# Five matmuls instead of six in units 2 and 14 of seven batches of a Fourier-mixing and maxout kernel

## The chip, the cores and the metric

The kernel runs on one core of one Trainium2 chip. The metric is the time of one execution on the device, in microseconds; runs of the kernel before took 401.41, 401.44 and 402.31 us, median 401.44. A core has a matrix engine (TensorE, PE in the profile, with its weight loads as PEld), a vector engine (VectorE, DVE), a scalar engine (ScalarE, ACT), GpSimd (POOL) and a queue engine for transfers (SyncE, SP). Each runs its own instructions in order, and they wait for one another by semaphores. Matmul results lie in PSUM, eight banks of 512 float32 columns by 128 partitions; all else lies in SBUF.

## What is computed

Eight batches of 3072 tokens with 256 features go through a two-dimensional Fourier transform, of which the real part is kept, and then through a layer that takes the largest of three products and a second matrix:

```python
batch, seq, dim = (8, 3072, 256)            # x; d_ff = 768
X = np.fft.fft(x, axis=1)
X = np.fft.fft(X, axis=2)
x = X.real.astype(np.float32).reshape(B * S, D)
h = np.maximum(np.maximum(x @ w1, x @ w2), x @ w3)
return h @ w_out
```

## The kernel before, in words

**Algebra.** The transform along the features is folded into the weights. For each batch the kernel makes two tables, tE and tO, of 128 rows by 1536 token columns (half the sequence; the other half are the mirrored tokens, which have the same even part and an odd part of the other sign). The weights w2 - w1 and w3 - w1 are kept transformed as gE and gO, so that pse = gE x tE + gO x tO is the first layer's difference for a token, and gD, which is gO times -2 with one row left out by the factor dif, turns it into the value for the mirrored token by one more product, pse + gD x tO. The hidden value is max(pse2, pse3, 0), and w1's part comes in later, as a linear term through gw.

**Units.** A batch has three blocks of 512 token columns and six groups (jc) of 128 hidden rows, so 18 units; the loop at the end runs over all 144 with one number g. A unit gives hp (tokens) and hm (mirrored tokens), 128 x 512 each in bf16. There are two kinds:
- Six matmuls: begin calls unit_plus (two products into pse2, two into pse3; L436, L437) and unit_out (ScalarE's Relu of pse2 into stmp, L450; VectorE's maximum with pse3 into hp, L451). finish calls unit_minus (one product with gD into each bank, L444) and unit_out again, into hm.
- Five matmuls ("split": odd g from 7 on). third, two units ahead, makes e3 = gE[1] x tE (L758) and d3 = gD[1] x tO (L760). ScalarE writes odd3 = -0.5 x d3 (L762), VectorE writes even3 = vb x wcol + e3 (L763; vb is row 0 of tO on all partitions), and POOL makes plus3 = even3 + odd3 and minus3 = even3 - odd3 in bf16 (L767). begin then makes pse2 alone (L774, L775), and VectorE takes max(pse2, 0, plus3) into hp (L776); finish adds gD[0] x tO (L444) and takes max(pse2, 0, minus3) into hm (L788).

**Order.** The order on every engine is the order of the program, written out by hand. In iteration g: if the unit before is split, its finish; then begin(g); then the finish of the unit before if it wasn't split; then third(g + 2) if g + 2 is split; scatter (POOL's indirect stores); ten steps of the second layer (l2_some: the products po and pl, L483 and L475, and hp and hm by w_out, L460, into po; then VectorE's ot = po + even, L488, and the stores); then what plan has for this unit of the next batch: the first transform (s, L369, evicted by ScalarE, L372) in units 1 and 2, the tables (k, L411, evicted by ScalarE, L413) in units 12 to 15, mirrored copies by ScalarE (L129), loads by POOL.

**Buffers.** PSUM is dealt out as: ps_f, a ring of three banks, which e3, d3, pl, the products of s and k, and a few others share; ps_l1, two banks for pse2; ps_w3, one bank for pse3 of even units; ps_o, two banks for po and for pse3 of odd units of six matmuls. s_pool holds three each of even3, odd3, plus3 and minus3; hp and hm have two sets, ot six.

Of the kernel before, what the change touches and what calls it, by code (L numbers as in the profile page):

```python
# [9 lines left out]
FP32 = mybir.dt.float32  # L10
BF16 = mybir.dt.bfloat16
INT32 = mybir.dt.int32
AX = mybir.ActivationFunctionType
ALU = mybir.AluOpType
# [36 lines left out]
def kernel(  # L51
# [9 lines left out]
    nc = tc.nc  # L61

    B, S, D = x.shape
# [3 lines left out]
    TOKB = 512  # L67
    NHALF = 1536
    UNITS = 3 * NJC
# [104 lines left out]
    for r in (0, 6, 11):  # L174
        n = {0: 6, 6: 5, 11: 4}[r]
# [25 lines left out]
    def scal(out, in0, s1, op0, s2=None, op1=None, eng=None):  # L201
# [8 lines left out]
                                   op0=ALU.mult, op1=ALU.add)  # L210
# [3 lines left out]
                                   op0=ALU.mult, op1=ALU.add)  # L214
# [5 lines left out]
                                   op0=ALU.mult, op1=ALU.add)  # L220
# [7 lines left out]
    half = gen.tile([128, 256], FP32, tag="half")  # L228
# [7 lines left out]
    for fc in range(2):  # L236
        scal(pf[:, fc:fc + 1], pidx, float(128 * fc), ALU.add)
        nc.vector.scalar_tensor_tensor(
            out=vm[:, fc * 256:(fc + 1) * 256].rearrange("p (k c) -> p k c", c=128),
            in0=dvec.unsqueeze(1).to_broadcast([128, 2, 128]), scalar=pf[:, fc:fc + 1],  # L240
            in1=half.rearrange("p (k c) -> p k c", c=128), op0=ALU.mult, op1=ALU.add)
# [12 lines left out]
                          in_=par.unsqueeze(1).to_broadcast([128, 2, 2]))  # L254
# [365 lines left out]
    for (s0, s1) in HALVES:  # L620
        for h in range(2):
            load_x(1, s0, s1, h)
        if s0 == 0:
            nc.gpsimd.dma_start(out=wout_bf.rearrange("p (jc c) -> p jc c", jc=NJC),
                                in_=moe_w_out.rearrange("(jc p) c -> p jc c", jc=NJC))
# [18 lines left out]
    for u in range(3):  # L644
# [7 lines left out]
                       in1=adj.unsqueeze(1).to_broadcast([128, B, 12]), op=ALU.add)  # L652
# [8 lines left out]
    s_pool = ctx.enter_context(tc.tile_pool(name="sums", bufs=3))  # L661
# [79 lines left out]

    sums = {}

    def is_split(g):
        return g % 2 == 1 and 7 <= g < B * UNITS

    def operands(g):
        b, u = divmod(g, UNITS)
        blk, jc = divmod(u, NJC)
        mm = mixes[b]  # L750
        ts = slice(blk * TOKB, (blk + 1) * TOKB)
        return slice(jc * 128, (jc + 1) * 128), mm.tE[:, ts], mm.tO[:, ts], mm.vb[:, ts], jc

    def third(g):

        js, te, to, vb, jc = operands(g)
        e3 = ps_f.tile([128, TOKB], FP32, name="e3", tag="ps")
        nc.tensor.matmul(e3, gE[1][:, js], te, start=True, stop=True)  # L758
        d3 = ps_f.tile([128, TOKB], FP32, name="d3", tag="ps")
        nc.tensor.matmul(d3, gD[1][:, js], to, start=True, stop=True)  # L760
        even3, odd3 = (s_pool.tile([128, TOKB], FP32, name=n, tag=n) for n in ("even3", "odd3"))
        nc.scalar.activation(out=odd3, in_=d3, func=AX.Copy, scale=-0.5)  # L762
        nc.vector.scalar_tensor_tensor(out=even3, in0=vb, scalar=wcol[:, jc:jc + 1], in1=e3,  # L763
                                       op0=ALU.mult, op1=ALU.add)
        sums[g] = [s_pool.tile([128, TOKB], BF16, name=n, tag=n) for n in ("plus3", "minus3")]
        for dst, op in zip(sums[g], (ALU.add, ALU.subtract)):
            nc.gpsimd.tensor_tensor(out=dst, in0=even3, in1=odd3, op=op)  # L767

    def begin(g, dst):

        js, te, to, _, jc = operands(g)
        if is_split(g):
            pse2 = ps_l1.tile([128, TOKB], FP32, name="pse2", tag="pse2")
            nc.tensor.matmul(pse2, gE[0][:, js], te, start=True, stop=False)  # L774
            nc.tensor.matmul(pse2, gO[0][:, js], to, start=False, stop=True)  # L775
            nc.vector.scalar_tensor_tensor(out=dst, in0=pse2, scalar=0.0, in1=sums[g][0],  # L776
                                           op0=ALU.max, op1=ALU.max)
            return (pse2,)
        pses = unit_plus(te, to, jc, TOKB, *((ps_o, "po") if g % 2 else (ps_w3, "pse3")))
        unit_out(pses, dst, TOKB)  # L780
        return pses

    def finish(g, pses, dst):

        js, te, to, _, jc = operands(g)
        unit_minus(pses, to, jc)
        if is_split(g):
            nc.vector.scalar_tensor_tensor(out=dst, in0=pses[0], scalar=0.0, in1=sums.pop(g)[1],  # L788
                                           op0=ALU.max, op1=ALU.max)
        else:  # L790
            unit_out(pses, dst, TOKB)

    prev = None
    for g in range(B * UNITS):
# [13 lines left out]
        if prev is not None and is_split(prev[0]):  # L808
            finish(*prev)
            prev = None  # L810
# [4 lines left out]
        for lead in (1, 2):  # L815
            if is_split(g + lead) and (lead == 1) == (g + lead == 7):
                third(g + lead)
# [46 lines left out]
```

## Time and profile before

| | us |
|---|---|
| median of three runs | 401.44 |
| the profiled execution | 403.04 |
| its span, first to last instruction | 400.8 |
| PE busy | 381.5 |
| DVE busy | 319.2 |
| POOL busy | 324.6 |
| ACT busy | 260.2 |

A row of the profile names the line of the kernel, the engine, the operation, the tile written and those read, their shapes, the count, then busy time and the mean of one. The main groups that the change touches, with the idle time just before them and what ended most of it:

```profile
L450 ACT ACTIVATE stmp<-pse 128x512 bf16<-128x512 f32 x150 | 89.8, 600 | 66.3 <-PE pse L444 46.3
L767 POOL TENSOR_TENSOR plus<-even,odd 128x512 bf16<-128x512 f32 x69 | 87.9, 1274 | 34.6 <-DVE even L763 28.4
L444 PE MATMUL pse<-tO,gD 128*128 128x512 bf16 x219 | 70.9, 379 | 0.6
L763 DVE SCALAR_TENSOR_TENSOR even<-vb,wcol,e 128x512 f32<-128x512 bf16 x69 | 51.0, 739 | 0.0
L762 ACT ACTIVATE odd<-d 128x512 f32<-128x512 f32 x69 | 41.3, 598 | 6.4 <-PE pl L475 0.4
```

A matmul's row is longer (379 ns) than the distance to the next one's start, because matmuls overlap in the array. Lines of the order of time give the start in us, the length in us, the engine, line, operation, tiles, and in brackets the engine's idle time before it with its releaser.

### The profile page before, as it was taken

The page shows a single profiled execution, that of the slowest core. Times are in us where ns is not written, and L with a number is a line of the kernel's source. Part 1 is how long each engine was busy: PE and PEld are TensorE (multiplying, and loading weights), DVE is VectorE, ACT ScalarE, POOL GpSimd, SP SyncE. Part 2 cuts the span into 40 slices and gives each one's busy share as a digit, 9 for nine tenths or more (in the row PEclk, how much of TensorE's full clock was granted, in tenths as well). Part 3 has the DMA queues.
Part 4 walks back from the last instruction along what each step waited for, and adds up shares of the span by engine and source line. Part 5 has one row for each costly group of instructions (what it writes and reads, how often), then busy time and mean ns, then how long its engine had stood idle before and what let it go on. Part 6 is the DMA issues. An engine that isn't in the chain of part 4 may idle for free.

```text
span 400.8 us, 8295 instructions
## 1 busy us (share of the span) xinstructions
PE 381.5 (95%) x2691; PEld 236.9 (59%) x2739; DVE 319.2 (80%) x542; ACT 260.2 (65%) x466; POOL 324.6 (81%) x408
## 2 busy tenths in 40 slices
PE   6679899999999999999999999999999999999994
PEld 2245456656665666656665666656665666666673
DVE  5978877877887887877887887877887887887982
ACT  1576779768865778568865778568775546544420
POOL 6465479788998899898988899898978798778993
PEclk9799999999999999999999999999999999999999
DMA  7989978395765958395875958394432653322234
GB/s 116 190 160 190 176 196 168 110 156 151 187 146 112 197 146 161 111 188 129 178 152 106 194 150 172 109 180 124 151 105 78 140 150 108 93 74 52 88 87 137
DMA packets 69532, 56.30 MB, mean 140 GB/s; under 512 B 35040, under 2 KB 64992, under 8 KB 68292
## 3 DMA queue, kind: packets, MB, share of 16 engines
q0 software_dynamic: 23552, 26.53, 35.4%
q1 hardware_dynamic: 44898, 28.70, 27.3%
q10 hardware_dynamic: 1040, 0.56, 0.5%
q8 instruction: 21, 0.34, 0.3%
q14 instruction: 21, 0.17, 0.2%
HBM read 38.15 MB, written 31.71 MB: 174 GB/s over the span
## 4 chain that ended last, share of the span: by engine, by line
PE 81%; DMA 8%; DVE 4%; ACT 3%; issue 2%; SPq 1%; POOL 0%; DVEq 0%; POOLq 0%; ACTq 0%
PE po L460 29%; PE pse L444 11%; PE pse L436 8%; PE pse L437 6%; PE po L483 4%; PE pse L774 4%; PE d L760 3%; PE e L758 3%; PE pse L775 3%; DMA yb<-db 3%; PE ps L369 3%; PE ps L411 2%; PE pl L475 2%; DMA xt<-in_x_dram 2%; ACT tb L372 2%
## 5 line engine op out<-in xcount | busy, mean ns | idle before, releaser
L450 ACT ACTIVATE stmp<-pse 128x512 bf16<-128x512 f32 x150 | 89.8, 600 | 66.3 <-PE pse L444 46.3
L570 POOL DMA_INDIRECT out_dram<-ot,rows_m x92 | 102.3, 1112 | 17.9 <-issue 7.8
L767 POOL TENSOR_TENSOR plus<-even,odd 128x512 bf16<-128x512 f32 x69 | 87.9, 1274 | 34.6 <-DVE even L763 28.4
L767 POOL TENSOR_TENSOR minus<-even,odd 128x512 bf16<-128x512 f32 x69 | 87.6, 1270 | 0.0
L460 PE MATMUL po<-wout_bf,hp 128*128 128x256 bf16 x576 | 86.1, 273 | 0.4
L776 DVE SCALAR_TENSOR_TENSOR hp<-pse,plus 128x512 bf16<-128x512 f32 x69 | 47.7, 691 | 46.1 <-PE pse L775 19.0
L460 PE MATMUL po<-wout_bf,hm 128*128 128x256 bf16 x576 | 78.6, 273 | 0.1
L460 PEld LDWEIGHTS <-hp 128*128 128x128 bf16 x576 | 56.4, 98 | 26.1
L444 PE MATMUL pse<-tO,gD 128*128 128x512 bf16 x219 | 70.9, 379 | 0.6
L460 PEld LDWEIGHTS <-hm 128*128 128x128 bf16 x576 | 56.4, 98 | 16.3
L488 DVE TENSOR_TENSOR ot<-po,even 128x512 f32<-128x512 f32 x92 | 63.0, 684 | 0.0
L451 DVE TENSOR_TENSOR hp<-pse,stmp 128x512 bf16<-128x512 f32 x75 | 51.6, 688 | 9.6 <-ACT stmp L450 7.8
L436 PE MATMUL pse<-tE,gE 128*128 128x512 bf16 x148 | 56.0, 378 | 2.0 <-DVE tE L413 0.5
L451 DVE TENSOR_TENSOR hm<-pse,stmp 128x512 bf16<-128x512 f32 x75 | 51.7, 689 | 7.2 <-ACT stmp L450 3.9
L763 DVE SCALAR_TENSOR_TENSOR even<-vb,wcol,e 128x512 f32<-128x512 bf16 x69 | 51.0, 739 | 0.0
L437 PE MATMUL pse<-tO,gO 128*128 128x512 bf16 x128 | 48.5, 379 | 0.2 <-issue 0.2
L788 DVE SCALAR_TENSOR_TENSOR hm<-pse,minus 128x512 bf16<-128x512 f32 x69 | 47.3, 685 | 1.2 <-PE pse L444 0.4
L762 ACT ACTIVATE odd<-d 128x512 f32<-128x512 f32 x69 | 41.3, 598 | 6.4 <-PE pl L475 0.4
L129 ACT COPY xt<-xt 64x762 bf16<-64x762 bf16 (+1 forms) x48 | 40.2, 838 | 1.1
L372 ACT CAST tb<-ps 128x512 bf16<-128x512 f32 x46 | 24.8, 589 | 22.9 <-PE ps L369 22.9
L444 PEld LDWEIGHTS <-gD 128*128 128x128 bf16 x219 | 21.4, 98 | 23.1 <-issue 5.0
L483 PE MATMUL po<-gw,tO 128*128 128x512 bf16 x86 | 32.7, 380 | 0.0
(156 smaller groups left out, 463.8 us busy)
## 6 DMA issues: line engine op xcount, KB each, us to landing
yb<-db SPq DMA_DIRECT2D x7, 833.0 KB
xt<-in_x_dram POOLq DMA_DIRECT2D x14, 384.0 KB, 8.6
out_dram<-ot SPq DMA_DIRECT2D x55, 96.0 KB
out_dram<-ot SPq DMA_DIRECT2D x64, 64.0 KB
db<-tb SPq DMA_DIRECT2D x21, 192.0 KB
vb<-vd SPq DMA_DIRECT2D x23, 128.0 KB
xt<-in_x_dram POOLq DMA_DIRECT2D x7, 400.0 KB, 8.6
xt<-in_x_dram POOLq DMA_DIRECT2D x7, 368.0 KB, 8.8
```

The source lines that it names most:

```text
L436: nc.tensor.matmul(pse[:, 0:n], gE[i][:, js], te, start=True, stop=False)
L437: nc.tensor.matmul(pse[:, 0:n], gO[i][:, js], to, start=False, stop=True)
L444: nc.tensor.matmul(pse, gD[i][:, js], to, start=False, stop=True, skip_group_check=True)
L450: nc.scalar.activation(out=stmp[:, 0:n], in_=pses[0][:, 0:n], func=AX.Relu)
L451: nc.vector.tensor_tensor(out=dst, in0=src3, in1=stmp[:, 0:n], op=ALU.max)
L460: nc.tensor.matmul(po, hcols(jc), wout_bf[:, jc * 256:(jc + 1) * 256], start=False, stop=(jc == NJC - 1), skip_group_check=True)
L483: nc.tensor.matmul(po, to[:, cp], gw[:, 256:768], start=True, stop=True)
L488: nc.vector.tensor_tensor(out=ot.rearrange("p (h c) -> p h c", h=2), in0=po.rearrange("p (h c) -> p h c", h=2), in1=lin.unsqueeze(1).to_br ...
L570: stored(nc.gpsimd.indirect_dma_start(out, bass.IndirectOffsetOnAxis(ap=rows_m[0:128 - lo, at_row: at_row + 1], axis=0), ot[lo:128, 256:51 ...
L763: nc.vector.scalar_tensor_tensor(out=even3, in0=vb, scalar=wcol[:, jc:jc + 1], in1=e3, op0=ALU.mult, op1=ALU.add)
L767: nc.gpsimd.tensor_tensor(out=dst, in0=even3, in1=odd3, op=op)
L776: nc.vector.scalar_tensor_tensor(out=dst, in0=pse2, scalar=0.0, in1=sums[g][0], op0=ALU.max, op1=ALU.max)
```

## The change

Units 2 and 14 of batches 1 to 7, 14 units in all, become units of five matmuls. They are even, so third runs for them in units 0 and 12, and from unit 1 to 3 and 13 to 15 three such units follow one another. For these units alone the sums are made otherwise: ScalarE's odd3 and POOL's two operations are left out, and VectorE makes plus3 = -0.5 x d3 + even3 and minus3 = 0.5 x d3 + even3 itself, reading d3 from its bank. Since is_split holds for them, their finish comes before the begin of the next unit, and they use no pse3 and no stmp.

```diff
+    def on_dve(g):
+        return g >= UNITS and g % UNITS in (2, 14) and g < B * UNITS
+
     def is_split(g):
-        return g % 2 == 1 and 7 <= g < B * UNITS
+        return (g % 2 == 1 and 7 <= g < B * UNITS) or on_dve(g)
...
-        even3, odd3 = (s_pool.tile([128, TOKB], FP32, name=n, tag=n) for n in ("even3", "odd3"))
-        nc.scalar.activation(out=odd3, in_=d3, func=AX.Copy, scale=-0.5)
+        even3 = s_pool.tile([128, TOKB], FP32, name="even3", tag="even3")
+        if not on_dve(g):
+            odd3 = s_pool.tile([128, TOKB], FP32, name="odd3", tag="odd3")
+            nc.scalar.activation(out=odd3, in_=d3, func=AX.Copy, scale=-0.5)
         nc.vector.scalar_tensor_tensor(out=even3, in0=vb, scalar=wcol[:, jc:jc + 1], in1=e3,
                                        op0=ALU.mult, op1=ALU.add)
         sums[g] = [s_pool.tile([128, TOKB], BF16, name=n, tag=n) for n in ("plus3", "minus3")]
+        if on_dve(g):
+            for dst, half in zip(sums[g], (-0.5, 0.5)):
+                nc.vector.scalar_tensor_tensor(out=dst, in0=d3, scalar=half, in1=even3,
+                                               op0=ALU.mult, op1=ALU.add)
+            return
         for dst, op in zip(sums[g], (ALU.add, ALU.subtract)):
             nc.gpsimd.tensor_tensor(out=dst, in0=even3, in1=odd3, op=op)
```

## What I expect, before the changed kernel has run

> **What bounds the kernel now.** I read the page's first table, then the chain of waits, then the sums over three batches, and last the order of time around the two places that the change touches.
>
> ```profile
> PE 381.5 (95%) x2691; PEld 236.9 (59%) x2739; DVE 319.2 (80%) x542; ACT 260.2 (65%) x466; POOL 324.6 (81%) x408
> ...
> PE 81%; DMA 8%; DVE 4%; ACT 3%; issue 2%; SPq 1%; POOL 0%; DVEq 0%; POOLq 0%; ACTq 0%
> ```
> ```profile
> 120.90:165.80 44.90, 44.58 (x319) 27.97 (x324) 36.45 (x58) 33.08 (x58) 39.63 (x47) 1.00 0.68 150
> 165.80:210.70 44.90, 44.58 (x319) 27.98 (x324) 36.60 (x58) 33.07 (x58) 39.60 (x47) 1.00 0.71 155
> ```
>
> The chain is TensorE's for 81%. The second block has two stretches of one batch each (length, then busy time of PE, PEld, DVE, ACT, POOL, then the granted clock): PE is busy for 44.58 of 44.90 us at full clock, VectorE for 36.5. A busy PE need not be a full one, so I look at the spacing of its starts:
>
> ```profile
> 120.92 0.81 PE L436 MATMUL pse<-tE,gE 128*128 128x512 bf16 x2
> 121.57 0.38 PE L437 MATMUL pse<-tO,gO 128*128 128x512 bf16 x1
> 121.78 0.38 PE L475 MATMUL pl<-gw,tE 128*128 128x256 bf16 x2
> ...
> 122.87 0.38 PE L774 MATMUL pse<-tE,gE 128*128 128x512 bf16 x1
> ...
> 123.95 0.38 PE L760 MATMUL d<-tO,gD 128*128 128x512 bf16 x1
> 124.17 0.82 PE L460 MATMUL po<-wout_bf,hm 128*128 128x256 bf16 x6
> ```
>
> This is unit 0 of batch 2 and the head of unit 1. Four matmuls of 512 columns (L436, L437) take 121.78 - 120.92 = 0.86 us, 0.215 each, and the rest follows without a hole. So the kernel is a stream of matmuls: one fewer is worth 0.215 us, and a wait of PE is paid in full.
>
> **What is removed.** A unit of six matmuls becomes one of five: 14 x 0.215 = 3.0 us less on the path. ScalarE's two Relu copies go (L450, 0.60 each; it is busy 33 of 44.9 us, so nothing for the end). POOL gets nothing, no DMA is added, and none is moved past another on SP's or POOL's queue. Stores whose ot comes later leave later; six ot buffers and POOL's 5 us of idle time a batch cover the 0.5 us that this is, which would show only at the last unit, and units 2 and 14 aren't last.
>
> **What is added on VectorE.** The unit's two outputs stay two instructions (L451 becomes L776 and L788, 0.69 for 0.69). New are the even sum and the two sums from the bank. VectorE's instructions overlap at their ends, so I count from start to start:
>
> ```profile
> 120.41 0.74 DVE L763 SCALAR_TENSOR_TENSOR even<-vb,wcol,e 128x512 f32<-128x512 bf16 x1
> 121.06 0.69 DVE L488 TENSOR_TENSOR ot<-po,even 128x512 f32<-128x512 f32 x1
> 121.66 0.68 DVE L788 SCALAR_TENSOR_TENSOR hm<-pse,minus 128x512 bf16<-128x512 f32 x1
> 122.26 0.68 DVE L451 TENSOR_TENSOR hp<-pse,stmp 128x512 bf16<-128x512 f32 x1
> 123.93 0.69 DVE L776 SCALAR_TENSOR_TENSOR hp<-pse,plus 128x512 bf16<-128x512 f32 x1 [0.99 <-PE pse L444]
> 124.54 0.68 DVE L451 TENSOR_TENSOR hm<-pse,stmp 128x512 bf16<-128x512 f32 x1
> ```
>
> The even sum holds the engine 0.65, the others 0.60. The new sums read a float32 bank, a float32 tile and a number, and write bf16. No row is quite that; the nearest are L776 (bank, number, bf16 out: 0.60, end after 0.69) and L763 (0.65, 0.74). I take 0.60 and 0.69, since L488 reads a float32 tile beside its bank in the same 0.60. Together 1.85 us a unit, 3.7 a batch: with 36.5 busy of 44.9 VectorE isn't full over a batch. It is full where the work falls. From 120.41 to 122.86 it has no hole, so the new work starts late, and PE needs its banks back.
>
> [...]
>
> **Place 1: unit 2, whose products are issued in unit 0.** Program order puts third(2) behind begin(0). PE: e3(2) at 121.78, d3(2) at 122.00, all that follows 0.43 later. VectorE: even3(2) starts behind hp(0), at 122.26 + 0.60 = 122.86, plus3 at 123.51, minus3 at 124.11, and that ends at 124.80. Only then is d3(2)'s bank free; before, ScalarE's copy (L762, 0.60) freed it as soon as the product stood. The ring has three banks; third(1), third(2), pl and third(3) take seven, so e3(3) and d3(3) take up the banks of even3(2) and minus3(2), whether banks go round in turn or in the order in which they came free. e3(3) at 123.74 + 0.43 = 124.17 finds its bank free (even3(2) ends at 123.60). d3(3) would start at 123.95 + 0.43 = 124.38 and must wait for minus3(2). What a release costs shows at another place: an ot that started at 191.60 and took 0.69 let L483 start at 192.34, 0.05 after its end. So d3(3) starts at 124.85: a wait of 0.47 us. Behind it in PE's queue stand the ten matmuls of the second layer and all after them. Later nothing is late: hp(1) starts at 124.71 instead of 123.93, but finish(1) asks for it only after 126.3; POOL's plus for unit 3 began at 126.80, when even3(3) will just be done. Net 0.47 - 0.215 = +0.255.
>
> **Place 2: unit 14, issued in unit 12.** Here the bank is asked for earlier, by the next batch's table product kO0 (L411):
>
> ```profile
> 151.50 0.38 PE L475 MATMUL pl<-gw,tE 128*128 128x256 bf16 x2
> ...
> 152.59 0.39 PE L411 MATMUL ps<-to_tab,yb 98*128 98x96 bf16 x6
> 152.84 0.38 PE L774 MATMUL pse<-tE,gE 128*128 128x512 bf16 x1
> ...
> 153.91 0.38 PE L760 MATMUL d<-tO,gD 128*128 128x512 bf16 x1
> ```
> ```profile
> 152.15 0.69 DVE L451 TENSOR_TENSOR hp<-pse,stmp 128x512 bf16<-128x512 f32 x1
> 153.54 0.69 DVE L776 SCALAR_TENSOR_TENSOR hp<-pse,plus 128x512 bf16<-128x512 f32 x1 [0.70 <-PE pse L775]
> ```
>
> Third(13) takes two banks, third(14) the third one and the first, pl the second, kO0 e3(14)'s. even3(14) runs behind hp(12), at 152.15 + 0.60 = 152.75, and ends at 153.49; kO0 would start at 152.59 + 0.43 = 153.02 and starts at 153.54: 0.52. Then e3(15) takes d3(14)'s bank. It is due 0.215 before d3(15), at 153.70 + 0.43 + 0.52 = 154.65; minus3(14) runs at 152.75 + 1.25 = 154.00, ends at 154.69, releases at 154.74: 0.09 more. Unit 14 itself now has its minus matmul ahead of begin(15), and hp(14) ends by my count 0.15 us before that matmul asks for it: no wait, but a thin cover, worth up to 0.1 each if it goes. Net 0.61 - 0.215 = +0.395. Batch 7 has no kO0; there the wait is as at place 1.
>
> **Sum.** 7 x 0.255 + 6 x 0.395 + 1 x 0.255 = 1.8 + 2.4 + 0.3 = +4.4 us. The profiled execution took 403.04 us (span 400.8 and 2.2 around it), the median of the runs is 401.44; the waits don't hang on that difference, so 401.44 + 4.4 = 405.8, and a profiled span near 405.2. With L763's 0.65 and 0.74 for both new sums minus3 ends 0.10 later: +1.4, 407.2. Bound below: PE waits nowhere, 398.4 (the next rival). Bound above: none of the 1.85 is hidden, 14 x (1.85 - 0.215) = +22.9, 424.3; I stay near the rows, as VectorE had 0.99 us of idle time right behind place 1 and 0.70 behind place 2.
>
> **Rivals.**
> (1) Faster: the banks come back in time and the 14 matmuls are simply gone: 401.44 - 3.0 = 398.4. Its place is d3(3) and kO0; it decides if VectorE reaches the new sums 0.5 us earlier than I count. For it: VectorE has a fifth of a batch idle and ScalarE is relieved. Against it: the run from 120.41 to 122.86 has no hole, and ends in hp(0), which waits for nothing by then but the engine.
> (2) Waits about as long as the saving: one of the two waits of a place is missing, or each is near 0.2 us: 14 x (0.2 - 0.215), 401.2; with the waits of place 2 alone missing, 8 x 0.255 - 6 x 0.215 = +0.75, 402.2. I give it 400.3 to 403.2. For it: the sum is a difference of small terms, each known to 0.1.
> (3) VectorE's queue becomes the bound for a few units: what isn't covered by the idle 0.99 behind place 1 lands on PE, 0.86 - 0.215 = 0.645 a place, x 14 = +9.0, 410.5, through finish(1), finish(14) or an ot that holds its po bank. For it: hp(14)'s cover of 0.15. Against: PE's demands lie a unit behind VectorE's answers elsewhere.
> (4) The change doesn't do what it says: 14 units would keep six matmuls; then 401.4. The condition in the diff is plain, so next to nothing.
>
> **How the numbers follow.** My forecast (403.2 to 408.5) 0.64, rival 1 0.13, rival 2 0.12, rival 3 0.10, rival 4 0.01. The measurement can tell about 0.3%, 1.2 us, from no change: rival 1 is faster, 0.13; of rival 2 two thirds and rival 4 are the same, 0.09; the rest slower, 0.78. The range runs from 400.5, which leaves rival 1 out, to 410.5, which leaves out half of rival 3. The likeliest one's own range is 403.2 to 408.5.
>
> **What would show it.** L436 and L437 lose 28 matmuls each, L444 loses 14; L758, L760, L774 and L775 gain 14 each (a few records of matmuls are missing in a trace). PE shows idle time before d (L760) or before a table product (L411) with DVE's minus3 or even3 as releaser, some 0.5 us at each place; a batch is 45.5 us long instead of 44.9; DVE is busy 14 x (0.74 + 2 x 0.69) = 30 us more in all, ACT 28 x 0.60 = 17 less. If those waits are absent and a batch is 44.5, rival 1 holds; if PE waits at L444 or L483 for hp or ot, rival 3. A longer stay of VectorE's new line than 0.69 would break the sum's size, not its sign.

## The result, and the profile after

The changed kernel takes 406.69 us (median of 6 runs, 404.68 to 407.47) beside 402.21 for the kernel before in the same comparison (401.41 to 403.07): a ratio of 1.0104, 95% interval 1.0081 to 1.0127, so 3.3 to 5.1 us slower. The profiled execution took 406.65 us, its span is 404.4 (before: 403.04 and 400.8). The forecast was 405.8. The sum came out; most of its terms did not. (A number in brackets behind a tile, as in hp(14), is the unit within its batch.)

From the page of the changed kernel, the busy time and the groups that answer to those shown before (line numbers have moved: L760 is now L763, L762 L767, L763 L768, L767 L777, L774 and L775 L784 and L785, L776 L786, L788 L798; the new sums are L773):

```profile
PE 382.0 (94%) x2725; PEld 235.1 (58%) x2725; DVE 342.4 (85%) x584; ACT 245.6 (61%) x438; POOL 324.8 (80%) x408
...
PE 75%; DVE 10%; DMA 7%; issue 3%; ACT 2%; POOL 1%; DVEq 0%; SPq 0%; POOLq 0%; ACTq 0%
...
L786 DVE SCALAR_TENSOR_TENSOR hp<-pse,plus 128x512 bf16<-128x512 f32 x83 | 56.8, 684 | 22.1 <-PE pse L785 9.8
L444 PE MATMUL pse<-tO,gD 128*128 128x512 bf16 x205 | 68.0, 379 | 4.2 <-DVE hp L786 2.9
```

L444 has 14 matmuls fewer and L786 14 instructions more, as announced. In the chain VectorE's share went from 4% to 10%. The new thing is in the last line: PE now stands idle before its minus matmul, and what ends the wait is VectorE's hp. Nothing on this page says that PE waited for a bank of the ring.

To see where the time lies I took from each trace the start of the weight load that opens unit 0 of each batch. The differences are the batches' lengths; for batch 7 the table gives the time to the same load of unit 17, in us:

| batch | 1 | 2 | 3 | 4 | 5 | 6 | 7 to unit 17 | batch 1 opens at |
|---|---|---|---|---|---|---|---|---|
| before | 44.90 | 44.89 | 44.89 | 44.90 | 45.28 | 44.88 | 40.51 | 75.81 |
| changed | 45.04 | 45.02 | 45.03 | 45.03 | 45.74 | 45.01 | 42.62 | 76.19 |

Six batches are 0.13 us longer each, batch 5 another 0.33, the last one 2.1: 3.2 us from the batches that the change touches. Another 0.4 was lost ahead of batch 1, where the programs don't differ; with it the two profiled executions are 3.6 us apart. The forecast had 0.65 a batch and 0.5 in the last.

**Batch 7.** The order of time in the changed kernel, unit 0 to the begin of unit 3 (VectorE from the sums of unit 2 on, then PE):

```profile
349.22 0.74 DVE L768 SCALAR_TENSOR_TENSOR even<-vb,wcol,e 128x512 f32<-128x512 bf16 x1
...
350.41 0.69 DVE L773 SCALAR_TENSOR_TENSOR plus<-d,even 128x512 bf16<-128x512 f32 x1 [0.46 <-PE pse L785]
...
351.02 0.68 DVE L773 SCALAR_TENSOR_TENSOR minus<-d,even 128x512 bf16<-128x512 f32 x1
...
351.62 0.68 DVE L786 SCALAR_TENSOR_TENSOR hp<-pse,plus 128x512 bf16<-128x512 f32 x1
...
352.21 0.68 DVE L451 TENSOR_TENSOR hm<-pse,stmp 128x512 bf16<-128x512 f32 x1
...
352.81 0.73 DVE L768 SCALAR_TENSOR_TENSOR even<-vb,wcol,e 128x512 f32<-128x512 bf16 x1
...
353.09 0.38 PE L785 MATMUL pse<-tO,gO 128*128 128x512 bf16 x1
...
353.47 0.68 DVE L488 TENSOR_TENSOR ot<-po,even 128x512 f32<-128x512 f32 x1
...
353.74 0.82 PE L460 MATMUL po<-wout_bf,hm 128*128 128x256 bf16 x6
...
354.18 0.68 DVE L798 SCALAR_TENSOR_TENSOR hm<-pse,minus 128x512 bf16<-128x512 f32 x1
354.78 0.68 DVE L786 SCALAR_TENSOR_TENSOR hp<-pse,plus 128x512 bf16<-128x512 f32 x1
...
355.51 0.38 PE L444 MATMUL pse<-tO,gD 128*128 128x512 bf16 x1 [0.95 <-DVE hp L786]
```

Unit 2's pse2 is complete once L785, which starts at 353.09, is done. Its hp waits in VectorE's queue behind everything that the sums pushed back and starts at 354.78. The minus matmul adds into the same bank and may not start before hp has been read: PE does its ten steps (the last six from 353.74 on) and then stands until 355.51, 0.05 after hp's end. In a unit of five matmuls the minus matmul comes ahead of the next begin, so nothing but those ten steps lies between. In the other batches the next batch's products lie there too (L369 in unit 2, L411 in unit 14) and cover the wait wholly or in part. Unit 14 of batch 7 shows the same wait:

```profile
385.46 0.38 PE L444 MATMUL pse<-tO,gD 128*128 128x512 bf16 x1 [1.15 <-DVE hp L786]
```

The bracket counts from the modelled end of the matmul before. Counted from the end of the last step by the spacing of the starts (0.109 a step), PE stood for some 1.1 us in unit 2 and 1.3 in unit 14. In unit 2 one more thing counts: plus3 waited for PE (0.46 in its bracket) and started 1.19 behind the even sum, where in the other 13 places it started 0.84 behind. VectorE has no hole from there to hp(2), so up to 0.35 of the 1.1 can come from that. Why it waits there is not known.

### The profile page after: what moved, and what is told of

It is laid out like the page before. It is cut to its first block, busy times and chain, and to the rows that moved or that the text cites. A ratio compares the mean times of both kernels' runs of the same rounds, so it can differ in the third digit from the quotient of the medians.

```text
span 404.4 us, 8299 instructions
## 1 busy us (share of the span) xinstructions
PE 382.0 (94%) x2725; PEld 235.1 (58%) x2725; DVE 342.4 (85%) x584; ACT 245.6 (61%) x438; POOL 324.8 (80%) x408
## 4 chain that ended last, share of the span: by engine, by line
PE 75%; DVE 10%; DMA 7%; issue 3%; ACT 2%; POOL 1%; DVEq 0%; SPq 0%; POOLq 0%; ACTq 0%
PE po L460 26%; PE pse L444 10%; PE pse L437 6%; PE pse L436 6%; PE po L483 4%; PE pse L784 4%; PE d L763 4%; PE e L761 4%; PE pse L785 4%; DMA yb<-db 3%; PE ps L369 3%; PE pl L475 2%; DMA xt<-in_x_dram 2%; DVE even L768 2%; DVE hp L786 2%
## 5 line engine op out<-in xcount | busy, mean ns | idle before, releaser
L777 POOL TENSOR_TENSOR plus<-even,odd 128x512 bf16<-128x512 f32 x69 | 87.7, 1271 | 38.9 <-DVE even L768 28.5
L450 ACT ACTIVATE stmp<-pse 128x512 bf16<-128x512 f32 x122 | 72.9, 598 | 63.2 <-PE pse L444 38.3
L777 POOL TENSOR_TENSOR minus<-even,odd 128x512 bf16<-128x512 f32 x69 | 87.5, 1269 | 0.0
L786 DVE SCALAR_TENSOR_TENSOR hp<-pse,plus 128x512 bf16<-128x512 f32 x83 | 56.8, 684 | 22.1 <-PE pse L785 9.8
L444 PE MATMUL pse<-tO,gD 128*128 128x512 bf16 x205 | 68.0, 379 | 4.2 <-DVE hp L786 2.9
L798 DVE SCALAR_TENSOR_TENSOR hm<-pse,minus 128x512 bf16<-128x512 f32 x83 | 56.7, 683 | 10.2 <-PE pse L444 10.2
L768 DVE SCALAR_TENSOR_TENSOR even<-vb,wcol,e 128x512 f32<-128x512 bf16 x83 | 61.1, 736 | 0.0
L767 ACT ACTIVATE odd<-d 128x512 f32<-128x512 f32 x69 | 41.2, 598 | 21.9 <-PE d L763 16.6
L451 DVE TENSOR_TENSOR hp<-pse,stmp 128x512 bf16<-128x512 f32 x61 | 41.8, 685 | 8.7 <-ACT stmp L450 7.6
L436 PE MATMUL pse<-tE,gE 128*128 128x512 bf16 x122 | 46.2, 378 | 1.0 <-DVE tE L413 0.5
L437 PE MATMUL pse<-tO,gO 128*128 128x512 bf16 x122 | 46.2, 379 | 0.0
L451 DVE TENSOR_TENSOR hm<-pse,stmp 128x512 bf16<-128x512 f32 x61 | 41.8, 685 | 2.3 <-ACT stmp L450 0.2
L372 ACT CAST tb<-ps 128x512 bf16<-128x512 f32 x46 | 24.8, 589 | 21.7 <-PE ps L369 21.5
L483 PE MATMUL po<-gw,tO 128*128 128x512 bf16 x92 | 34.9, 380 | 0.0
L444 PEld LDWEIGHTS <-gD 128*128 128x128 bf16 x205 | 20.0, 98 | 21.3 <-issue 6.5
```

Of the source, the lines that this page charges most:

```text
L436: nc.tensor.matmul(pse[:, 0:n], gE[i][:, js], te, start=True, stop=False)
L437: nc.tensor.matmul(pse[:, 0:n], gO[i][:, js], to, start=False, stop=True)
L444: nc.tensor.matmul(pse, gD[i][:, js], to, start=False, stop=True, skip_group_check=True)
L450: nc.scalar.activation(out=stmp[:, 0:n], in_=pses[0][:, 0:n], func=AX.Relu)
L451: nc.vector.tensor_tensor(out=dst, in0=src3, in1=stmp[:, 0:n], op=ALU.max)
```

## The experiments

Theory A: VectorE's queue is late with hp, and PE pays at finish(2) and finish(14) what no matmul covers. Theory B, the forecast's: PE pays at the ring of three banks, evenly over the batches. All edits are to the changed kernel.

**Leave batch 7 alone.**

```diff
-        return g >= UNITS and g % UNITS in (2, 14) and g < B * UNITS
+        return UNITS <= g < (B - 1) * UNITS and g % UNITS in (2, 14)
```

> Units 2 and 14 take five matmuls in batches 1 to 6 alone; batch 7 is as before. Theory A (the time is lost where finish(2) and finish(14) wait for hp, and batch 7 has no matmuls of a next batch between begin and finish to cover it): batch 7 took 2.1 of the 3.6 us between the two profiled executions, so about 406.7 - 2.1 = 404.6, and batch 7 as long as before (44.5). Theory B (the forecast: waits for the ring's banks, spread evenly): 2 places of 0.255 less, 406.2.

Measured: 403.96 us, 1.0053 of before (1.0023 to 1.0083). Batch 7 is back at 40.51, batches 1 to 4 stay at 45.04. As A has it: the larger part of the loss, 2.1 of the 3.2 us of the batches, lay in two units of one batch.

**The minus matmul behind the next begin.**

```diff
-        if prev is not None and is_split(prev[0]):
+        if prev is not None and is_split(prev[0]) and not on_dve(prev[0]):
```

> The changed kernel, but the minus matmul of units 2 and 14 comes behind the begin of the next unit, as it does for units of six matmuls. Theory A: the two matmuls of begin cover 0.43 us of the wait for hp: the 0.28 at unit 14 of six batches goes, and 0.43 of each of the two waits in batch 7: 406.7 - 6 x 0.28 - 2 x 0.43 = 404.2. Theory B: waits for banks don't ask for the finish: 406.7, within 0.3.

Measured: 401.97 us, 1.0008 of before (0.9978 to 1.0038). The same matmuls and the same instructions on VectorE, one place in the order changed: batches 1 to 4 take 44.76, 0.13 less than before instead of 0.13 more, batch 7 41.76 instead of 42.62. Over the seven batches that is 2.6 us less than in the changed kernel, A's 2.5; that the median fell by nearly 5 is not from there (in the profiled execution batch 1 opened at 74.29 instead of 76.19). Batch 7 is still 1.25 longer than before: there PE now stands at begin(3) and begin(15), because VectorE is late with hm(1) and hm(13) as well (total us, times, longest):

```profile
PE pse L784 <- DVE hm L798: 0.9, 2, 0.6
```

In this run, at unit 14 of batch 3 (the table product, the two matmuls of begin(15), then the minus matmul of unit 14):

```profile
200.82 0.68 DVE L786 SCALAR_TENSOR_TENSOR hp<-pse,plus 128x512 bf16<-128x512 f32 x1
201.04 0.39 PE L411 MATMUL ps<-te_tab,yb 98*128 98x64 bf16 x6
201.27 0.38 PE L784 MATMUL pse<-tE,gE 128*128 128x512 bf16 x1
...
201.49 0.38 PE L785 MATMUL pse<-tO,gO 128*128 128x512 bf16 x1
201.71 0.38 PE L444 MATMUL pse<-tO,gD 128*128 128x512 bf16 x1
```

hp starts at 200.82 and ends at 201.50; the minus matmul comes at 201.71 without waiting. In the changed kernel at the same place it had to wait:

```profile
203.27 0.68 DVE L786 SCALAR_TENSOR_TENSOR hp<-pse,plus 128x512 bf16<-128x512 f32 x1
203.49 0.39 PE L411 MATMUL ps<-te_tab,yb 98*128 98x64 bf16 x6
...
204.00 0.38 PE L444 MATMUL pse<-tO,gD 128*128 128x512 bf16 x1
```

L411's six products take 0.23 (201.04 to 201.27 above), so PE was free at 203.72 and stood for 0.28.

**One sum less, one sum more.** The first run makes plus3 alone and reads it for hm too, the second makes minus3 twice:

```diff
+            sums[g] = [sums[g][0]] * 2
-            for dst, half in zip(sums[g], (-0.5, 0.5)):
+            for dst, half in zip(sums[g][:1], (-0.5,)):
```
```diff
-            for dst, half in zip(sums[g], (-0.5, 0.5)):
+            for dst, half in zip(sums[g] + sums[g][1:], (-0.5, 0.5, 0.5)):
```

> Leaves out the second sum of units 2 and 14: plus3 is used for hm too, so VectorE has one instruction of 0.60 us less at each place. Theory A: hp is 0.60 earlier: unit 14's waits of 0.28 go in six batches and 0.6 of each wait in batch 7: 406.7 - 1.7 - 1.2 = 403.8, the rest of the wait stays at L444 in batch 7. Theory B: d3's bank is free 0.6 earlier: 8 x 0.47 + 6 x 0.09 = 4.3 less, 402.4, and no waits at L444.

> The changed kernel with minus3 of units 2 and 14 made twice: 0.60 us more on VectorE at each place. Theory A (hp behind VectorE's queue): the wait at finish(14) grows by 0.6 in six batches, that at finish(2) by 0.5 (0.1 of cover was left), both waits of batch 7 by 0.6: 406.7 + 3.6 + 3.0 + 1.2 = 414.5, all of it before L444. Theory B (the ring): the bank of d3 comes back 0.6 later and PE waits for it before L763, L369 or L411, not before L444.

Measured: 402.16 us with one sum less (1.0009 of before, 0.9973 to 1.0044) and 413.09 with one more (1.0262, 1.0240 to 1.0285). With one sum less the total is better than A's 403.8 and near B's 402.4, but batch 1 opened at 74.37, 1.8 us earlier than in the changed kernel, so it doesn't tell the theories apart. Batches 1 to 4 take 44.70, 0.33 less (A: 0.28), but not for A's reason alone. In unit 13 of batch 3 d3(15) no longer waits:

```profile
196.51 0.69 DVE L775 SCALAR_TENSOR_TENSOR plus<-d,even 128x512 bf16<-128x512 f32 x1
...
197.05 0.38 PE L761 MATMUL e<-tE,gE 128*128 128x512 bf16 x1
...
197.26 0.38 PE L763 MATMUL d<-tO,gD 128*128 128x512 bf16 x1
```

It starts 0.21 behind e3(15), when plus3(14) has ended (197.20), while in the changed kernel it started 0.43 behind. That is a wait for a bank of the ring, 0.21 of the 0.33. The wait for hp(14) fell from 0.28 to 0.14 and didn't go, as A had it. That the sum of the two fits A is luck; this run shows something of both theories. In batch 7 (1.17 less; A: 1.2) a wait of 0.67 is left at L444 in unit 14, where the same bracket has 1.15 in the changed kernel, and in unit 2 plus3 started 0.84 behind the even sum.

With one sum more, batches take some 46.3, about 1.25 longer than in the changed kernel where A had 1.1, and batch 7 is 1.45 longer (A: 1.2). From the waits of the two kernels, the changed one first, then the one with a sum more (total us, times, longest):

```profile
PE pse L444 <- DVE hp L786: 2.9, 4, 1.1
```
```profile
PE pse L444 <- DVE hp L786: 11.7, 16, 1.3
```

The waits before L444 grow by 8.8 us, in front of the matmul where A has them. That the batches grow by more than A had fits the second minus3, which writes the same tile: it starts 0.71 behind the first, not 0.60.

**Cover in batch 7.**

```diff
-        l2_some(10)
+        l2_some({2: 16, 3: 4, 14: 16, 15: 4}.get(u, 10) if b == B - 1 else 10)
```

> The changed kernel; in batch 7, six of the second layer's ten steps of units 3 and 15 are done in units 2 and 14, between begin and finish: 0.65 us of matmuls as cover. Theory A: both waits of batch 7 shrink by 0.65 and nothing is paid later: 406.7 - 1.3 = 405.4, batch 7 about 0.8 longer than before instead of 2.1. If it is VectorE's work as a whole that batch 7 can't take, not the place of the wait, the time comes back in units 3 and 15: 406.7.

Measured: 405.01 us, 1.0060 of before (1.0043 to 1.0076); batch 7 takes 41.59, 1.03 less than in the changed kernel where I had 1.3. Work that is there anyway, put between begin and finish, takes the wait's place. Unit 2 is 0.66 shorter, as expected; of the wait there 0.30 is left, where the same bracket had 0.95:

```profile
353.48 0.68 DVE L786 SCALAR_TENSOR_TENSOR hp<-pse,plus 128x512 bf16<-128x512 f32 x1
...
354.22 0.38 PE L444 MATMUL pse<-tO,gD 128*128 128x512 bf16 x1 [0.30 <-DVE hp L786]
```

Unit 14 gains 0.37 alone: an ot now stands ahead of hm(14) in VectorE's queue, and 0.28 comes back one unit later, as a wait of the minus matmul for hp(15).

**The sums on POOL, as in the other units of five matmuls.**

```diff
-        if not on_dve(g):
-            odd3 = s_pool.tile([128, TOKB], FP32, name="odd3", tag="odd3")
-            nc.scalar.activation(out=odd3, in_=d3, func=AX.Copy, scale=-0.5)
+        odd3 = s_pool.tile([128, TOKB], FP32, name="odd3", tag="odd3")
+        nc.scalar.activation(out=odd3, in_=d3, func=AX.Copy, scale=-0.5)
...
-        if on_dve(g):
...
-            return
```

> Units 2 and 14 take five matmuls, but their sums are made as in all other such units: ScalarE's odd3, POOL's plus3 and minus3. VectorE has 1.4 us less at each place than in the changed kernel, POOL 2.5 us more. If VectorE's queue is what makes hp late (theory A) and POOL keeps up: the waits at L444 go, 406.7 - 1.7 - 2.3 = 402.7 or less. If POOL's queue is then the later one (5.1 us more a batch on 5.3 us of idle time): hp waits for plus3, 406 or more, with VectorE's waits ended by POOL.

Measured: 414.14 us, 1.0312 of before (1.0277 to 1.0347), far above either figure. One batch of it (length, busy time of PE, PEld, DVE, ACT, POOL), and the longest wait of hp over the whole run (total us, times, longest):

```profile
124.24:171.30 47.06, 45.21 (x324) 27.87 (x322) 37.42 (x60) 31.95 (x56) 44.63 (x52) 1.00 0.67 145
```
```profile
DVE hp L780 <- POOL plus L771: 27.8, 25, 2.2
```

POOL is busy for 44.6 of 47.1 us, and hp waits 27.8 us in all for its plus, where it was 14.5 in the kernel before: POOL, not VectorE, then sets a batch. That is what taking the sums on VectorE avoids. Batch 6, in which POOL has less to do, is the test without that limit:

```profile
311.33:355.96 44.63, 44.63 (x325) 27.83 (x323) 37.62 (x60) 24.99 (x47) 41.39 (x48) 1.00 0.45 118
```

It takes 44.63, beside 44.88 before and 45.01 in the changed kernel: with the sums off VectorE and POOL not full, the same five matmuls pay. (It doesn't tell the theories apart: ScalarE then frees d3's bank as well.)

**Two versions meant to beat both.** The first puts the two edits above together (batches 1 to 6, minus matmul behind begin). The second also moves ScalarE's last mirrored copy from unit 12 to unit 11:

```diff
-            at(b - 2, 5 + ch + 3 * (b == 2), lambda b=b, ch=ch: turn(b, ch))
+            at(b - 2, 5 + min(ch, 6) + 3 * (b == 2), lambda b=b, ch=ch: turn(b, ch))
```

> Five matmuls in units 2 and 14 of batches 1 to 6 alone, and their minus matmul behind the next begin. From the traces of the runs so far: 0.13 us less a batch, batch 7 as before: 0.8 us less than before, 400.8 where before is 401.6.

> As the one before, and ScalarE's last mirrored copy (L129) goes from unit 12 to unit 11, so that kO0 is evicted at once: d3(15) took kO0's bank and waited 0.215 us for that eviction. If so, 6 x 0.215 = 1.3 us less again, 399.5. If the copy is then in the way of stmp in unit 11, the gain is gone: 400.8 or more.

Measured: 401.72 us beside 402.50, 0.9990 (0.9966 to 1.0015), and 403.26, 1.0034 (1.0005 to 1.0063). The first has batches of 44.76 and batch 7 at 40.51 as expected, but 0.8 us can't be told from nothing in whole runs. In the second the gain was given back. d3(15) no longer waits (it starts 0.21 behind e3(15)), PE arrives earlier at unit 15, and there it waits for VectorE twice; from the order of time of that kernel in batch 3:

```profile
203.54 0.68 DVE L798 SCALAR_TENSOR_TENSOR hm<-pse,minus 128x512 bf16<-128x512 f32 x1
203.75 0.39 PE L411 MATMUL ps<-te_tab,yb 98*128 98x64 bf16 x6
204.14 0.68 DVE L786 SCALAR_TENSOR_TENSOR hp<-pse,plus 128x512 bf16<-128x512 f32 x1
...
204.28 0.38 PE L784 MATMUL pse<-tE,gE 128*128 128x512 bf16 x1
204.49 0.38 PE L785 MATMUL pse<-tO,gO 128*128 128x512 bf16 x1
204.87 0.38 PE L444 MATMUL pse<-tO,gD 128*128 128x512 bf16 x1
```

begin(15) writes the bank of unit 13 and starts at 204.28, when hm(13) (203.54, 0.68 long) has been read; the minus matmul starts at 204.87, when hp(14) (204.14) has. 0.30 and 0.16 us, more than the 0.21 saved at d3(15). Its batches are 45.09 long.

## Why the prediction was right in size and wrong in place

**The stream of matmuls: right.** A matmul is worth 0.215 us, and its removal shows: in the changed kernel, and in the one with the late minus matmul, place 1 gains 0.13, which is 0.215 less a new wait of 0.09 before d3(5) (in batch 2 of the changed kernel ScalarE's copies L372 end at 130.23 and d3(5) starts at 130.28).

**Place 1, "d3(3) must wait for minus3(2)": wrong.** The changed kernel at that place, in batch 2:

```profile
124.22 0.69 DVE L773 SCALAR_TENSOR_TENSOR plus<-d,even 128x512 bf16<-128x512 f32 x1
...
124.69 0.38 PE L761 MATMUL e<-tE,gE 128*128 128x512 bf16 x1
124.83 0.68 DVE L773 SCALAR_TENSOR_TENSOR minus<-d,even 128x512 bf16<-128x512 f32 x1
124.91 0.38 PE L763 MATMUL d<-tO,gD 128*128 128x512 bf16 x1
```

d3(3) starts 0.22 behind e3(3), while minus3(2) still runs. So it lies in another bank than d3(2). No trace names a bank; that third(3) has the banks of pl and e3(2), and that d3(2)'s goes to the first product of s, which comes 1.4 us later, is my reading, and the times agree with it: ScalarE's copy of pl, issued later, is done before the even sum (123.75 and 124.12), and e3(3) starts behind both. I had written that it made no difference whether banks go in turn or by release; by this reading it does. The 0.47 doesn't exist, and neither does the 0.52 at kO0, which in batch 3 starts at 198.45 while the even sum of unit 14 still runs (198.17 to 198.90), and so isn't in e3(14)'s bank. Place 1 alone gains: -0.13 where I had +0.255.

**Place 2: +0.27 for +0.395, by other waits.** d3(15) waited 0.21 and started 0.05 after the end of kO0's eviction (199.93), which ScalarE began 0.5 late behind the mirrored copy (so PE did pay at the ring, but at another product, by another engine); the minus matmul of unit 14 waited 0.28 for hp(14), where I had a cover of 0.15. From batch 3:

```profile
198.39 0.93 ACT L129 COPY xt<-xt 64x889 bf16<-64x889 bf16 x1
198.45 0.39 PE L411 MATMUL ps<-to_tab,yb 98*128 98x96 bf16 x6
...
199.34 0.59 ACT L413 CAST tO<-ps 128x512 bf16<-128x512 f32 x1
...
199.55 0.38 PE L761 MATMUL e<-tE,gE 128*128 128x512 bf16 x1
...
199.98 0.38 PE L763 MATMUL d<-tO,gD 128*128 128x512 bf16 x1
```

**The three sums: 2.05 us, not 1.85.** plus3 starts 0.84 behind even3 in 13 of 14 places, not 0.65: it reads what even3 writes, and waits for its end (0.74) and 0.10 more. plus3 to minus3 is 0.61, minus3 to the next 0.60, durations 0.69 and 0.68, as taken. VectorE's busy time rose by 23 us where 30 was announced: the 30 added up row lengths (all of VectorE's rows add up to 347.0 us before and 375.9 in the changed kernel), while its busy time (319.2 and 342.4) counts overlapping ends once.

**Batch 7 "as at place 1": wrong, and it is more than half of the loss.** Units 2 and 14 cost +0.90 and +1.21 there, not 0.255 each (0.215 gained; waits of some 1.1 and 1.3 for hp, and 0.12 at d3(15)). This is the third rival's mechanism, VectorE's queue as the bound for a few units with finish(2) or finish(14) as the place, to which I gave 0.10. It was priced evenly, 0.645 at all fourteen; in fact it depends on what lies between begin and finish: 0.7 us of products in unit 2 of six batches (no wait), 0.23 in unit 14 (0.28), nothing in batch 7 (some 1.1 and 1.3). That the minus matmul comes ahead of the next begin stood in the forecast; that PE then has no begin to do before it asks for hp was not followed up. The run with that one line changed shows it as the cause of 2.6 us. The rest of batch 7's loss stays VectorE's, at begin instead of finish.

**The sum.** +4.4 forecast, 3.6 between the two profiled executions, 3.3 to 5.1 in the runs. That the forecast lies so near is luck: two waits that weren't there stood in for others, elsewhere. By the traces 14 matmuls less give -3.0; the waits are 0.5 before d3(5) and 1.3 before d3(15) in six batches, 1.7 before the minus matmul of unit 14 there, and 2.5 in batch 7. That makes 3.0, beside 2.9 by the batches' lengths without batch 5's extra 0.33.

That 0.33 is another matter. Among batches 1 to 6, in batch 5 alone and in all ten profiled executions, ScalarE stands in unit 12 at L404 until the transfer into yb has landed; the kernel before and the changed one:

```profile
286.74 0.27 ACT L404 COPY yb<-x0s 98x17 bf16<-98x17 bf16 x1 [1.01 <-DMA yb<-db]
```
```profile
287.60 0.27 ACT L404 COPY yb<-x0s 98x17 bf16<-98x17 bf16 x1 [1.07 <-DMA yb<-db]
```

Everything behind it on ScalarE is late, and kO0 with it. The wait differs from execution to execution, and the batch's excess over its neighbours with it: 0.58 and 0.06 us with one sum less, 1.92 and 1.9 with the copy moved. Why the transfer lands when it does is not settled.

## What to carry to other kernels

A matmul (0.215 us) saved by work on another engine paid here only where the answer of that engine was covered at the point where the matrix engine asks for it (0.13 gained at place 1 of six batches, 1.21 lost in unit 14 of batch 7): count what lies in its queue between the product and the next use of the same bank, in every stage, and above all in the last one, which has no work of a next batch to put in between. Before changing the amount of work, look at the order: one condition put two matmuls ahead of a wait and was worth 2.6 us of the 3.2 that the batches had lost. When a wait is taken away upstream, check that the time doesn't return at the next request to the same late engine.

## What the runs showed of the hardware that I had not expected

In the traces two VectorE instructions of 512 columns overlapped at their ends, 0.60 from start to start at a length of 0.69; where plus3 reads the even sum's result the distance was 0.84 for a first of 0.74. And batch 1 opened between 74.3 and 77.5 us over ten profiled executions, with the same instructions up to there in all but the version with the moved copy: that scatter is as large as what was to be measured, so the batches' lengths, which in the two kernels agree to 0.02 us over batches 1 to 4, tell small differences apart that whole runs don't.
